# Turned keys in half a zeroed tile, z turned in five pieces, and another order of passes, scores and extra products

## The chip, the cores and the metric

The kernel runs on one core of one Trainium2 chip. The metric is the device time of one execution in microseconds. Names of the engines as the profile writes them: PE is TensorE (its weight loads are PEld), DVE is VectorE, ACT is ScalarE, POOL is GpSimd, and SP is SyncE, which here only issues DMAs.

## The reference

There are 8 batches of S = 3200 rows; u and v have D = 256 columns, z has 64. For every batch two stages follow each other:

```python
scores = (1.0 / S) * z @ z.T                 # S x S, symmetric
attn   = np.maximum(scores, 0.0) ** 2
x      = u * (attn @ v)                      # S x 256
wq, wk = x @ w_q, x @ w_k                    # S x 64 each
W_tok  = (1.0 / 8) * wq @ wk.T               # S x S, no nonlinearity
mixed  = W_tok @ x
out    = np.maximum(mixed, 0.0) @ w_out      # S x 256, float32
```

Since nothing stands between W_tok and x, the kernel computes wk.T @ x first (64 x 256, called the heads), and then wq times that.

## The kernel before

**Tiling.** The rows of a batch are 25 tiles of 128, put together in 7 groups: six of 512 rows and a last one of 128 (number 6, LASTG). For a group, the first stage makes score tiles (128 rows t by 512 columns of the group), squares them into fp16 tiles `at`, and multiplies them with v. As the scores are symmetric, a block that another group of the batch needs too is not computed again but turned by a transposing DMA (`tt`, `ttl`).

**Phases.** The main loop (`while groups`) runs through phases k = 0 to 164. An ordinary phase makes six score tiles, in three pairs, ahead of their use (LAG is two phases), and consumes some of the rows t of the current group: `second_product` lists the products that add up in two accumulator banks, acc0 and acc1. A group takes one to five phases. When it closes, `gate` multiplies the banks with u to give x and has x turned by a DMA. The last group of a batch is "split": its rows are shared out to the two banks, whose sum is taken in the gate (L391 to L393).

**Lanes.** Most phases run their products "on lanes" (`lanes`, L293 is where each product is emitted): the contraction over 128 rows is cut into a lower and an upper half of 64 rows, and two products, one from each half of PE, run side by side. A pass goes once through a set of products, with the lower lane in one bank and the upper lane in the other; the second pass goes through them with the lanes changed round. Between the passes `swap_after` waits for the ends of the first.

**PSUM.** There are the two accumulator banks and a pool of three tiles of two banks each ("ps"), which serves score pairs (sc), products for keys (qk), mixing products (mx) and projections (fo). The pool hands out the slot that was given back first. A slot is free again when the engines that read it are done.

**Score pairs.** A pair is evicted with ReLU by DVE (L243) or ACT (L239) into g, and g is squared into `at` by POOL (L258) or ACT (L256) in the next phase. In a phase the first two pairs stand at the head ("head scores") and the last one stands between the first and the second passes ("between score", `between_`).

**Extra products.** A phase can carry one extra:

- A key product (`keys_and_heads`): w_q and w_k times the turned x of a group, into the first bank of a qk tile, and beside it, in the second bank, the heads: turned keys of the group before (kx) times its x. ACT casts the first bank to fp16 (L432), SP issues the DMA that turns the keys (`turn_keys`), and DVE adds the heads to their sum (`heads_out`, L478 to L487). At the end of a batch the last two groups go together (a second cast, ql). A product of the batch before for its last 128 rows can go along as a "side product" (`aside`), read by ACT into rs or fs (L622, L641).
- A projection (`project`): mixed times w_out, evicted by ACT (L598) and written out.

`key_due` says when a key product may run, `mix_due` when a mixing product may. In a phase in which a group begins, the extra's first pass comes ahead of the banks' first pass; in others behind it. Its second pass comes ahead of the banks' second pass in both.

**Keys.** The DMA writes the turned keys into one half of a kx tile (128 rows x 4 x 2 x 64); POOL copies that half into the other (L454, `double_keys`), so that the heads come out twice, on partitions 0 to 63 and on 64 to 127. The copy is issued on POOL in the phase of the next key product, ahead of that phase's squares. The mixing products take the heads from both halves of the partitions.

**z.** For the next batch, POOL's queue loads z, DVE doubles it (`double_z`), and one transposing DMA, issued on SP, turns all 25 tiles (`turn_z`).

**Order.** Every engine runs its instructions in the order in which the program emits them; nothing is rescheduled. SP issues all transposing DMAs, the loads of u and the stores, POOL's queue loads z and v.

Of the kernel before, what the change touches and what calls it, by code (L numbers as in the profile page):

```python
# [9 lines left out]
FP16 = mybir.dt.float16  # L10
FP32 = mybir.dt.float32
# [5 lines left out]
def kernel(  # L17
# [10 lines left out]
    nc = tc.nc  # L28

    B, S, D = u.shape  # L30
    dqk = z.shape[2]
    dh = moe_w_q.shape[1]
# [21 lines left out]
    pzt = ctx.enter_context(tc.tile_pool(name="pzt", bufs=2))  # L54
    pv = ctx.enter_context(tc.tile_pool(name="pv", bufs=2))
    px = ctx.enter_context(tc.tile_pool(name="px", bufs=5))
    pk = ctx.enter_context(tc.tile_pool(name="pk", bufs=3))
    pxt = ctx.enter_context(tc.tile_pool(name="pxt", bufs=3))
    pu = ctx.enter_context(tc.tile_pool(name="pu", bufs=2))
    pg = ctx.enter_context(tc.tile_pool(name="pg", bufs=8))  # L60
# [36 lines left out]
    def load_first_v(n0, nn):  # L97
        nc.gpsimd.dma_start(out=vs[0][:, n0 : n0 + nn, :], in_=rows(v, 0)[:, n0 : n0 + nn, :])
# [34 lines left out]
    def double_z(b):  # L133
        nc.vector.tensor_copy(out=zds[b][:, :, 1, :], in_=zds[b][:, :, 0, :])

    def turn_z(b):
        zT[b] = pzt.tile([P, S], FP16, tag="zT2", name="zT2")
        nc.sync.dma_start_transpose(
            out=zT[b][:].rearrange("p (n s) -> p n s", s=P),
            in_=zds.pop(b)[:].rearrange("p n a k -> p (n a k)"),  # L140
        )

    def load_u(b, gi):
# [9 lines left out]
    wk2 = consts.tile([P, ND, 2, dh], FP32, tag="wk2", name="wk2")  # L153
    wo = consts.tile([P, ND, D], FP16, tag="wo", name="wo")
    zeros = consts.tile([P, D], FP16, tag="zeros", name="zeros")
    raw = {}

    def load_weights():
# [4 lines left out]
        nc.sync.dma_start(out=raw["k"], in_=moe_w_k.rearrange("(c p) h -> p c h", p=P))  # L163
        nc.sync.dma_start(out=raw["o"][:], in_=moe_w_out.rearrange("(c p) e -> p c e", p=P))

    def cast_weights():
        nc.gpsimd.tensor_copy(out=wqk[:, :, 0, :], in_=raw["q"])
        nc.gpsimd.tensor_copy(out=wqk[:, :, 1, :], in_=raw["k"])
        nc.gpsimd.tensor_copy(out=wkq[:, :, 1, :], in_=raw["q"])
        nc.gpsimd.tensor_copy(out=wkq[:, :, 0, :], in_=raw["k"])  # L170
        nc.gpsimd.memset(zeros[:], 0.0)
        for tile_ in hz:
            nc.gpsimd.memset(tile_[0:dh, :], 0.0)
        for half in range(2):
            nc.gpsimd.tensor_copy(out=wq2[:, :, half, :], in_=raw["q"])
            nc.gpsimd.tensor_copy(out=wk2[:, :, half, :], in_=raw["k"])
        nc.gpsimd.tensor_copy(out=wo[:], in_=raw["o"][:])

    LASTG = NG - 1

# [197 lines left out]
    def gate(b, gi):  # L383
        nn = widths[gi] // P
        xs[b, gi] = px.tile([P, 4, D], FP16, tag="x_sb", name="x_sb")
        x = xs[b, gi][:].rearrange("p n d -> p (n d)")
        ug = us.pop((b, gi))[:].rearrange("p n d -> p (n d)")
        n = min(2, nn) * D
        if is_split(b, gi):
            both = pg.tile([P, W], FP32, tag="g", name="gt")  # L390
            nc.scalar.copy(out=both[:, 0:n], in_=accs[1][:, 0:n])  # L391
            nc.vector.tensor_add(out=both[:, 0:n], in0=accs[0][:, 0:n], in1=both[:, 0:n])
            nc.vector.tensor_mul(out=x[:, 0:n], in0=both[:, 0:n], in1=ug[:, 0:n])  # L393
        else:
            if nn > 2:
                upper = pg.tile([P, W], FP32, tag="g", name="gt")
                nc.scalar.copy(out=upper[:], in_=accs[1][:])  # L397
            nc.vector.tensor_mul(out=x[:, 0:n], in0=accs[0][:, 0:n], in1=ug[:, 0:n])  # L398
            if nn > 2:
                nc.vector.tensor_mul(out=x[:, n : 2 * n], in0=upper[:], in1=ug[:, n : 2 * n])  # L400
        turn_x(b, gi)
# [32 lines left out]
    def turn_keys(b, gi):  # L434
        gw = widths[gi]
        mine = slice(0, dh) if swapped(gi) else slice(dh, P)
        ks[b, gi] = pk.tile([P, 4, 2, dh], FP16, tag="kx", name="kx")
        nc.sync.dma_start_transpose(
            out=ks[b, gi][:, 0 : gw // P, 1, :],
            in_=qks[b, gi][mine, 0:gw],  # L440
        )

    doubled = set()

    def double_keyed():
        hb, hgis = keyed[0]
        for g_ in hgis:
            if (hb, g_) not in doubled:
                doubled.add((hb, g_))
                double_keys(hb, g_)  # L450

    def double_keys(b, gi):
        nn = widths[gi] // P
        nc.gpsimd.tensor_copy(out=ks[b, gi][:, 0:nn, 0, :], in_=ks[b, gi][:, 0:nn, 1, :])  # L454

    def swapped(gi):
        return gi % 2 == 1 or gi == LASTG
# [15 lines left out]
    def heads_out(b, gis, ps):  # L475
        if gis[0] == 0:
            hacc[b] = psml.tile([P, D], FP32, tag="ha", name="ha")
            nc.vector.tensor_copy(out=hacc[b][:], in_=ps[:, 1, 0:D])  # L478
        elif gis[-1] < LASTG:
            nc.vector.tensor_add(out=hacc[b][:], in0=hacc[b][:], in1=ps[:, 1, 0:D])  # L480
        else:
            heads_done(b, ps[:, 1, 0:D])
            nc.vector.tensor_copy(out=hz[b % 2][dh:P, :], in_=hss[b][dh:P, :])

    def heads_done(b, part):
        hss[b] = psml.tile([P, D], FP16, tag="hs", name="hs")
        nc.vector.tensor_add(out=hss[b][:], in0=hacc.pop(b)[:], in1=part)  # L487

    def last_gram(b, gi, ps):
        nj = widths[gi] // P  # L490
# [158 lines left out]
    def due(k, fn):  # L649
        at_phase.setdefault(k, []).append(fn)  # L650
# [53 lines left out]
    def group_begun(k, b, gi):  # L704
        if gi + 1 < NG:
            due(k + 1, lambda: load_u(b, gi + 1))
        elif b + 1 < B:
            due(k + 1, lambda: load_u(b + 1, 0))
        if gi == 0 and b + 1 < B:
            later = 4 if b == 0 else 0  # L710
            due(k + later + 3, lambda: load_z(b + 1))
            due(k + later + 9, lambda: double_z(b + 1))
            due(k + later + 10, lambda: turn_z(b + 1))
            for i in range(5):
                due(k + later + 5 + 3 * i, lambda i=i: load_v(b + 1, 5 * i, 5))

# [3 lines left out]
    make_identity(nc, ident)  # L720
    load_first_z()
    load_first_v(0, 4)
    cast_first(0)
    turn_first(0)
    cast_first(1)
# [3 lines left out]
    load_first_v(18, 7)  # L729
    load_first_v(4, 8)  # L730
    due(3, lambda: load_u(0, 0))
    due(5, load_weights)
    due(8, cast_weights)

    def mix_due(k):
        if todo_mix and todo_mix[0][2] == 0 and len(todo_proj) > 2:
# [4 lines left out]
        return (older or len(todo_mix) > 2) and k - mixed_at[0] >= 2 and not key_due(k)  # L741

    def key_due(k):
        between_ = 2 if len(groups) > NG else 1
        return todo_between and todo_between[0][0] <= k and k - keyed_at[0] > between_

    made_by = []
    waiting = []
# [4 lines left out]
    while groups:  # L753
# [16 lines left out]
        n = min(n, NTILE - produced)  # L770
        pairs = list(range(produced, produced + n, 2))
        on_lanes = k >= 3 and len(pairs) + bool(mixing) >= 2
        between_ = [pairs.pop()] if on_lanes else []
        fresh = [(p0, scores(p0)) for p0 in pairs]
        produced += n
        made_by.append(produced)
        keying = not mixing and key_due(k)
        if keying and keyed:
            double_keyed()
        if mixing:  # L780
            mix_out(*mixing)
        staged = []
# [29 lines left out]
            continue  # L812
        ready = made_by[k - (1 if k < 3 else LAG)]
        b, gi = groups[0]
        begins = left is None
        if begins:
            group_begun(k, b, gi)
            need = ends[b, gi]
# [23 lines left out]
        extra = None  # L842
        if keying:
            extra = todo_between.pop(0)[1]()
        elif todo_proj and (mixing or begins or len(groups) <= NG) and (b, gi) != (last, LASTG):
            extra = project(*todo_proj.pop(0))
        if mixing and mixing[2] == 1:
            todo_proj.extend((mixing[0], 2 * mixing[1] + a) for a in range(2))
        if on_lanes:
            split = is_split(b, gi)  # L850
            if extra and not all(extra[0]):
                for fn in whole(extra[0]):
                    fn()
                extra[1]()
                extra = None
            if extra and begins:
                ends_ = lanes(extra[0], across, False)
            if split:
                both_lanes(banks)
            else:  # L860
                ends_ = lanes(banks, across, False)
            if extra and not begins:
                ends_ = lanes(extra[0], across, False)
            for x in acts[1:]:
                second_stage(*x)
            for p0 in between_:
                stage(p0, scores(p0))
            if extra or not split:
                swap_after(ends_)
                across = not across  # L870
            if extra:
                lanes(extra[0], across, True)
                extra[1]()
            if not split:
                lanes(banks, across, True)
        else:
            assert not is_split(b, gi)
            matmuls = whole(banks)
            cut = 10 if extra else 0
            if closes and (b, gi) == (last, LASTG):  # L880
                assert not extra
                cut = 20
                psg = [acc_tile(1, "xtx")[:, 0:D], ps_tile("xtx")[:, 0, 0:D]]
                extra = [], lambda: last_gram(last, LASTG - 1, psg)
            for fn in matmuls[:cut]:
                fn()
            if extra:
                for fn in whole(extra[0]):
                    fn()
                extra[1]()  # L890
            for x in acts[1:]:
                second_stage(*x)
            for fn in matmuls[cut:]:
                fn()
# [22 lines left out]

    halves = [(True, nc.sync, 2), (True, nc.sync, 2)]

    double_keyed()  # L920
    hb, hgis = keyed.pop()
    psh = ps_tile("hd")
    for fn in whole([heads(hb, hgis, psh, stop=False)]):
# [60 lines left out]
```

## Time and profile before

| | |
|---|---|
| time, three runs | 800.03, 806.02, 813.67 us (median 806.02) |
| time of the profiled execution | 810.74 us |
| its span, first to last instruction | 809.0 us |
| mean granted clock of PE | 0.994 |
| PE busy | 770.5 us, 95% |
| DVE, ACT, POOL busy | 506.1, 485.3, 481.3 us |
| DMA moved | 141.70 MB, mean 175 GB/s |
| transposing DMAs issued on SP (tt, xT, kx, zT) | 162, 56, 47, 7 for the larger kinds |

"Busy" is the time in which the engine has an instruction under way. Matmuls are pipelined and their ends are modelled, so 95% means that PE hardly ever stops, not that its array is full. The groups of instructions give the source line, the engine, the operation, the tile written and the one read, the shape, the number of them, their busy time and the mean of one in ns, and behind the bar the time that the engine stood idle just before them, with what released it. A line of the timeline gives the start and the length in us, and in brackets the wait before it.

### The profile page before, as it was taken

What the parts mean: (1) busy time and instruction counts of PE and PEld (TensorE: products, weight loads), DVE (VectorE), ACT (ScalarE), POOL (GpSimd) and SP (SyncE); (2) the same over time, 40 slices, a digit from 0 to 9 for tenths busy, and PEclk for the clock granted to TensorE, in tenths of its full rate; (3) what the DMA queues carried; (4) which work ended last, traced back from release to release, by engine and by line L of the source; (5) the groups of instructions that cost most, each with busy time, mean ns of one, the idle gap of its engine ahead of it and who ended that gap; (6) DMA issues with size and microseconds to landing.
All of it is one profiled execution on the core that took longest, in us unless ns stands there. A gap on an engine that the chain in (4) does not pass through costs nothing. (4 is left out here: it accounts for less than half of the span.)

```text
span 809.0 us, 27835 instructions
## 1 busy us (share of the span) xinstructions
PE 770.5 (95%) x12338; PEld 624.5 (77%) x12338; DVE 506.1 (63%) x516; ACT 485.3 (60%) x569; POOL 481.3 (59%) x351
## 2 busy tenths in 40 slices
PE   7889999999999999899999899999999989999996
PEld 4667877887788778788778677878878868778884
DVE  5765567656676567655767556765567645676524
ACT  6654566557576557555666546755666645665634
POOL 7865677646765567645676365663767545766520
PEclk9999999999999999999999999999999999999999
DMA  8999799999999969999899969999999995999826
GB/s 161 159 186 195 142 169 173 182 175 158 192 176 214 160 138 186 161 198 227 162 190 174 190 135 177 155 187 222 188 195 160 184 183 132 194 188 161 194 55 229
DMA packets 331159, 141.70 MB, mean 175 GB/s; under 512 B 310560, under 2 KB 313248, under 8 KB 331040
## 3 DMA queue, kind: packets, MB, share of 16 engines
q1 hardware_dynamic: 302768, 123.70, 83.5%
q0 software_dynamic: 28128, 15.98, 17.6%
q8 instruction: 96, 1.57, 0.8%
q10 hardware_dynamic: 144, 0.26, 0.1%
q14 instruction: 23, 0.19, 0.1%
HBM read 59.38 MB, written 26.21 MB: 106 GB/s over the span
## 5 line engine op out<-in xcount | busy, mean ns | idle before, releaser
L258 POOL TENSOR_TENSOR at<-g 128x1024 f16<-128x1024 f32 (+1 forms) x228 | 421.7, 1857 | 204.7 <-DVE g L243 148.6
L243 DVE TENSOR_SCALAR g<-sc 128x1024 f32<-128x1024 f32 (+1 forms) x330 | 389.3, 1187 | 235.0 <-PE sc L220 230.2
L293 PE MATMUL acc<-v_sb,at 64*128 64x256 f16 (+1 forms) x6995 | 443.3, 270 | 8.1 <-DVE x_sb L398 2.5
L293 PEld LDWEIGHTS <-at 64*128 64x128 f16 (+1 forms) x6995 | 353.7, 94 | 89.9 <-PE acc L293 17.0
L256 ACT ACTIVATE at<-g 128x1024 f16<-128x1024 f32 (+2 forms) x224 | 224.5, 1031 | 1.5 <-DMA ttl<-at 0.9
L239 ACT ACTIVATE g<-sc 128x1024 f32<-128x1024 f32 x122 | 125.2, 1026 | 115.8 <-PE sc L220 115.7
L293 PE MATMUL acc<-v_sb,tt 64*128 64x256 f16 (+1 forms) x2528 | 170.2, 270 | 0.0
L220 PE MATMUL sc<-zT 64*128 64x512 f16 x888 | 154.4, 380 | 5.6 <-DVE g L243 4.2
L293 PEld LDWEIGHTS <-tt 64*128 64x128 f16 (+1 forms) x2528 | 128.1, 94 | 12.8
L454 POOL COPY kx<-kx 128x256 f16<-128x256 f16 (+1 forms) x54 | 22.5, 421 | 94.0 <-DMA kx<-qk 90.3
L397 ACT COPY gt<-acc 128x512 f32<-128x512 f32 x48 | 28.1, 585 | 71.4 <-PE acc L293 68.9
L293 PE MATMUL qk<-x_sb,kx 64*128 64x256 f16 x378 | 57.8, 275 | 11.4 <-POOL kx L454 11.4
L598 ACT ACTIVATE fo<-fo 128x1024 f32<-128x1024 f32 (+2 forms) x44 | 43.7, 999 | 34.5 <-PE fo L293 34.0
L537 ACT ACTIVATE rt<-mx 128x1024 f16<-128x1024 f32 x47 | 47.9, 1025 | 25.4 <-PE mx L516 23.5
L432 ACT CAST qk<-qk 128x512 f16<-128x512 f32 x47 | 27.5, 584 | 54.5 <-PE qk L293 54.0
L220 PEld LDWEIGHTS <-zT 64*128 64x128 f16 x888 | 49.7, 94 | 13.4 <-issue 6.8
L293 PE MATMUL fo<-wo,rt 64*128 64x256 f16 (+1 forms) x704 | 56.9, 271 | 0.1
L398 DVE TENSOR_TENSOR x_sb<-acc,u_sb 128x512 f16<-128x512 f32 (+1 forms) x49 | 33.6, 686 | 37.3 <-PE acc L293 36.5
L293 PEld LDWEIGHTS <-kx 64*128 64x128 f16 (+1 forms) x382 | 32.1, 95 | 23.1 <-POOL kx L454 14.3
L293 PEld LDWEIGHTS <-rt 64*128 64x128 f16 (+1 forms) x704 | 34.8, 94 | 18.4 <-PE acc L293 4.4
L400 DVE TENSOR_TENSOR x_sb<-gt,u_sb 128x512 f16<-128x512 f32 x48 | 43.0, 895 | 2.4 <-ACT gt L397 2.2
L293 PE MATMUL qk<-xT_sb,wqk 64*128 64x512 f16 (+1 forms) x92 | 32.7, 395 | 1.6 <-DMA xT_sb<-x_sb 1.6
(68 smaller groups left out, 269.6 us busy)
## 6 DMA issues: line engine op xcount, KB each, us to landing
u_sb<-in_u_dram SPq DMA_DIRECT2D x48, 512.0 KB, 5.0
out_dram<-fo SPq DMA_DIRECT2D x45, 512.0 KB, 4.1
v_sb<-in_v_dram POOLq DMA_DIRECT2D x35, 320.0 KB, 5.5
zd<-in_z_dram POOLq DMA_DIRECT2D x7, 400.0 KB, 10.7
tt<-at SPq DMA_TRANSPOSE x162, 4.9
out_dram<-fo SPq DMA_DIRECT2D x5, 256.0 KB, 2.7
u_sb<-in_u_dram SPq DMA_DIRECT2D x8, 128.0 KB, 3.6
xT_sb<-x_sb SPq DMA_TRANSPOSE x56, 4.5
```

What stands on the lines that cost most here:

```text
L220: nc.tensor.matmul(out=sc[:, h, :], lhsT=zT[b][half : half + dqk, ts(ti, P)], rhs=zT[b][half : half + dqk, ds(gs, W)], start=True, stop=True,)
L239: nc.scalar.activation(out=g[:, hs, 0:w], in_=sc[:, hs, W - w : W], func=RELU, scale=GSCALE)
L243: nc.vector.tensor_scalar(out=g[:, hs, 0:w], in0=sc[:, hs, W - w : W], scalar1=0.0, scalar2=GSCALE, op0=AOP.max, op1=AOP.mult,)
L256: nc.scalar.square(out=out, in_=g[:, hs, 0:w])
L258: nc.gpsimd.tensor_mul(out=out, in0=g[:, hs, 0:w], in1=g[:, hs, 0:w])
L293: return nc.tensor.matmul(out=self.out, lhsT=self.lhsT(rows), rhs=self.rhs(rows), start=start, stop=stop)
L397: nc.scalar.copy(out=upper[:], in_=accs[1][:])
L398: nc.vector.tensor_mul(out=x[:, 0:n], in0=accs[0][:, 0:n], in1=ug[:, 0:n])
L400: nc.vector.tensor_mul(out=x[:, n : 2 * n], in0=upper[:], in1=ug[:, n : 2 * n])
L432: nc.scalar.copy(out=qks[b, gi][:, 0:gw], in_=out)
L537: nc.scalar.activation(out=out, in_=ps[:], func=RELU)
L598: nc.scalar.mul(out=flat_out[:, sl], in_=part, mul=FINAL_SCALE)
```

## The change

- `turn_keys`: three fixed kx tiles are set to zero once, at the start. The DMA writes the turned keys into half 0 of a tile, and half 1 stays zero. The copy on POOL is gone. The heads then come out on partitions 0 to 63 alone; the running sum is kept there, and DVE copies the finished one, `hs`, to partitions 64 to 127, once a batch.
- `turn_z`: five DMAs of five tiles each, in five phases in a row, take the place of one.
- The weights are loaded in phase 4 instead of 5, and their casts on POOL are spread over phases 8, 10, 11 and 13.
- The gate of a split group has DVE copy acc0 into SBUF, and adds from there.
- `key_due` and the choice of projections follow other conditions.
- Ordinary phases with no extra and no group start have one head pair and two between pairs; a mixing phase without extra has none and two.
- On lanes, all first passes come first, then the between scores, then the second passes in the same order as the first. So in a phase in which a group begins the extra is ahead in both; in any other it is behind the banks in both. In a split group the first ten rows of both banks come ahead of the between scores and the others behind them.

```diff
-    def turn_z(b):
-        zT[b] = pzt.tile([P, S], FP16, tag="zT2", name="zT2")
+    def turn_z(b, n0, nn):
+        if n0 == 0:
+            zT[b] = pzt.tile([P, S], FP16, tag="zT2", name="zT2")
         nc.sync.dma_start_transpose(
-            out=zT[b][:].rearrange("p (n s) -> p n s", s=P),
-            in_=zds.pop(b)[:].rearrange("p n a k -> p (n a k)"),
+            out=zT[b][:].rearrange("p (n s) -> p n s", s=P)[:, n0 : n0 + nn, :],
+            in_=zds[b][:, n0 : n0 + nn, :, :].rearrange("p n a k -> p (n a k)"),
         )
...
+    kxs = [pk.tile([P, 4, 2, dh], FP16, tag=f"kx{i}", name=f"kx{i}") for i in range(3)]
...
+    def clear():
+        for tile_ in [zeros] + kxs:
+            nc.gpsimd.memset(tile_[:], 0.0)
...
-            both = pg.tile([P, W], FP32, tag="g", name="gt")
-            nc.scalar.copy(out=both[:, 0:n], in_=accs[1][:, 0:n])
-            nc.vector.tensor_add(out=both[:, 0:n], in0=accs[0][:, 0:n], in1=both[:, 0:n])
-            nc.vector.tensor_mul(out=x[:, 0:n], in0=both[:, 0:n], in1=ug[:, 0:n])
+            both = pg.tile([P, 2, W], FP32, tag="g", name="gt")
+            nc.scalar.copy(out=both[:, 1, 0:n], in_=accs[1][:, 0:n])
+            nc.vector.tensor_copy(out=both[:, 0, 0:n], in_=accs[0][:, 0:n])
+            nc.vector.tensor_add(out=both[:, 0, 0:n], in0=both[:, 0, 0:n], in1=both[:, 1, 0:n])
+            nc.vector.tensor_mul(out=x[:, 0:n], in0=both[:, 0, 0:n], in1=ug[:, 0:n])
...
-        ks[b, gi] = pk.tile([P, 4, 2, dh], FP16, tag="kx", name="kx")
+        kxs.append(kxs.pop(0))
+        ks[b, gi] = kxs[-1]
         nc.sync.dma_start_transpose(
-            out=ks[b, gi][:, 0 : gw // P, 1, :],
+            out=ks[b, gi][:, 0 : gw // P, 0, :],
...
-    def double_keys(b, gi):
-        nn = widths[gi] // P
-        nc.gpsimd.tensor_copy(out=ks[b, gi][:, 0:nn, 0, :], in_=ks[b, gi][:, 0:nn, 1, :])
...
-        nc.vector.tensor_add(out=hss[b][:], in0=hacc.pop(b)[:], in1=part)
+        nc.vector.tensor_add(out=hss[b][0:dh, :], in0=hacc.pop(b)[0:dh, :], in1=part[0:dh, :])
+        nc.vector.tensor_copy(out=hss[b][dh:P, :], in_=hss[b][0:dh, :])
...
-            due(k + later + 10, lambda: turn_z(b + 1))
+            for i in range(5):
+                due(k + later + 10 + i, lambda i=i: turn_z(b + 1, 5 * i, 5))
...
     def key_due(k):
-        between_ = 2 if len(groups) > NG else 1
-        return todo_between and todo_between[0][0] <= k and k - keyed_at[0] > between_
+        late = len(groups) <= NG
+        if not todo_between or k - keyed_at[0] <= (1 if late else 2):
+            return False
+        ready = todo_between[0][0]
+        if late or todo_proj:
+            return ready <= k
+        if left is None:
+            return ready - 1 <= k
+        return ready <= k and not (len(sizes) < 3 and k + len(sizes) - ready < 3)
...
-        between_ = [pairs.pop()] if on_lanes else []
+        keying = not mixing and key_due(k)
+        begins = left is None
+        projecting = not keying and todo_proj and groups[0] != (last, LASTG) and (
+            begins or len(todo_proj) > (1 if mixing else 2) or len(groups) <= NG
+        )
+        heading = len(pairs)
+        if on_lanes:
+            heading = heading - 1 if begins or keying or projecting else 1 - bool(mixing)
+        between_ = pairs[heading:]
+        pairs = pairs[:heading]
...
-            if extra and begins:
-                ends_ = lanes(extra[0], across, False)
-            if split:
-                both_lanes(banks)
-            else:
-                ends_ = lanes(banks, across, False)
-            if extra and not begins:
-                ends_ = lanes(extra[0], across, False)
+            parts = [] if split else [banks]
+            if extra:
+                parts.insert(0 if begins else len(parts), extra[0])
+            cut = 10
+            firsts = [lanes(part, across, False) for part in parts]
+            if split:
+                both_lanes([bank[:cut] for bank in banks])
             for x in acts[1:]:
                 second_stage(*x)
             for p0 in between_:
                 stage(p0, scores(p0))
-            if extra or not split:
+            if split:
+                both_lanes([bank[cut:] for bank in banks])
+            if parts:
+                across = not across
+            for part, ends_ in zip(parts, firsts):
                 swap_after(ends_)
-                across = not across
-            if extra:
-                lanes(extra[0], across, True)
-                extra[1]()
-            if not split:
-                lanes(banks, across, True)
+                lanes(part, across, True)
+                if extra and part is extra[0]:
+                    extra[1]()
```

More of the change, by code (lines that the diff above doesn't have):

```diff
@@ L56 @@
     px = ctx.enter_context(tc.tile_pool(name="px", bufs=5))
-    pk = ctx.enter_context(tc.tile_pool(name="pk", bufs=3))
+    pk = ctx.enter_context(tc.tile_pool(name="pk", bufs=1))
     pxt = ctx.enter_context(tc.tile_pool(name="pxt", bufs=3))
@@ L164, in load_weights @@
         nc.sync.dma_start(out=raw["o"][:], in_=moe_w_out.rearrange("(c p) e -> p c e", p=P))
+    def clear():
+        for tile_ in [zeros] + kxs:
+            nc.gpsimd.memset(tile_[:], 0.0)
+        for tile_ in hz:
+            nc.gpsimd.memset(tile_[0:dh, :], 0.0)
     def cast_weights():
@@ L170, in cast_weights, with double_weights, cast_out_weights @@
         nc.gpsimd.tensor_copy(out=wkq[:, :, 0, :], in_=raw["k"])
[L171 to L176, printed above, removed]
+    def double_weights(half):
+        nc.gpsimd.tensor_copy(out=wq2[:, :, half, :], in_=raw["q"])
+        nc.gpsimd.tensor_copy(out=wk2[:, :, half, :], in_=raw["k"])
+    def cast_out_weights():
         nc.gpsimd.tensor_copy(out=wo[:], in_=raw["o"][:])
@@ L436, in turn_keys @@
         mine = slice(0, dh) if swapped(gi) else slice(dh, P)
-        ks[b, gi] = pk.tile([P, 4, 2, dh], FP16, tag="kx", name="kx")
+        kxs.append(kxs.pop(0))
+        ks[b, gi] = kxs[-1]
         nc.sync.dma_start_transpose(
-            out=ks[b, gi][:, 0 : gw // P, 1, :],
+            out=ks[b, gi][:, 0 : gw // P, 0, :],
             in_=qks[b, gi][mine, 0:gw],
         )
[L443 to L450, printed above, removed]
-    def double_keys(b, gi):
-        nn = widths[gi] // P
-        nc.gpsimd.tensor_copy(out=ks[b, gi][:, 0:nn, 0, :], in_=ks[b, gi][:, 0:nn, 1, :])
     def swapped(gi):
@@ L477, in heads_out @@
             hacc[b] = psml.tile([P, D], FP32, tag="ha", name="ha")
-            nc.vector.tensor_copy(out=hacc[b][:], in_=ps[:, 1, 0:D])
+            nc.vector.tensor_copy(out=hacc[b][0:dh, :], in_=ps[0:dh, 1, 0:D])
         elif gis[-1] < LASTG:
-            nc.vector.tensor_add(out=hacc[b][:], in0=hacc[b][:], in1=ps[:, 1, 0:D])
+            nc.vector.tensor_add(
+                out=hacc[b][0:dh, :], in0=hacc[b][0:dh, :], in1=ps[0:dh, 1, 0:D]
+            )
         else:
             heads_done(b, ps[:, 1, 0:D])
-            nc.vector.tensor_copy(out=hz[b % 2][dh:P, :], in_=hss[b][dh:P, :])
+            nc.vector.tensor_copy(out=hz[b % 2][dh:P, :], in_=hss[b][0:dh, :])
     def heads_done(b, part):
         hss[b] = psml.tile([P, D], FP16, tag="hs", name="hs")
-        nc.vector.tensor_add(out=hss[b][:], in0=hacc.pop(b)[:], in1=part)
+        nc.vector.tensor_add(out=hss[b][0:dh, :], in0=hacc.pop(b)[0:dh, :], in1=part[0:dh, :])
+        nc.vector.tensor_copy(out=hss[b][dh:P, :], in_=hss[b][0:dh, :])
     def last_gram(b, gi, ps):
@@ L722 @@
     load_first_v(0, 4)
+    clear()
     cast_first(0)
@@ L731 @@
     due(3, lambda: load_u(0, 0))
-    due(5, load_weights)
+    due(4, load_weights)
     due(8, cast_weights)
+    due(10, lambda: double_weights(0))
+    due(11, lambda: double_weights(1))
+    due(13, cast_out_weights)
     def mix_due(k):
@@ L772 @@
         on_lanes = k >= 3 and len(pairs) + bool(mixing) >= 2
-        between_ = [pairs.pop()] if on_lanes else []
+        keying = not mixing and key_due(k)
+        begins = left is None
+        projecting = not keying and todo_proj and groups[0] != (last, LASTG) and (
+            begins or len(todo_proj) > (1 if mixing else 2) or len(groups) <= NG
+        )
+        heading = len(pairs)
[3 more added lines that the diff above has]
+        pairs = pairs[:heading]
         fresh = [(p0, scores(p0)) for p0 in pairs]
@@ L776 @@
         made_by.append(produced)
-        keying = not mixing and key_due(k)
-        if keying and keyed:
-            double_keyed()
         if mixing:
@@ L814 @@
         b, gi = groups[0]
-        begins = left is None
         if begins:
@@ L844 @@
             extra = todo_between.pop(0)[1]()
-        elif todo_proj and (mixing or begins or len(groups) <= NG) and (b, gi) != (last, LASTG):
+        elif projecting:
             extra = project(*todo_proj.pop(0))
```

1 line of the change is left out of this document (removed).

## The prediction, made before the changed kernel was run

> **What bounds the kernel now.** I read the busy shares first, then the table of waits, then stretches of the timeline.
>
> ```profile
> PE 770.5 (95%) x12338; PEld 624.5 (77%) x12338; DVE 506.1 (63%) x516; ACT 485.3 (60%) x569; POOL 481.3 (59%) x351
> ...
> DMA  8999799999999969999899969999999995999826
> ```
>
> TensorE (PE) is the bound (the DMA row, busy tenths in 40 slices, comes back under rival 3). Two lanes finish a product of 256 columns every 0.109 us; at that pace the products need 749 us of the 799 us between the first and the last. The other 50 us are pauses, and only what makes or removes a pause of PE counts. In the table of waits (who waits for whom: total us, times, longest):
>
> ```profile
> POOL kx L454 <- DMA kx<-qk: 90.3, 21, 10.9
> ...
> ACT gt L397 <- PE acc L293: 68.9, 46, 4.2
> ...
> PE qk L293 <- POOL kx L454: 11.4, 8, 2.8
> ...
> PE sc L220 <- DVE g L243: 4.2, 6, 0.7
> ```
>
> The first row is large and free: POOL waits, PE doesn't. PE's own waits are the last two rows, some 0.5 us at each of the 16 group starts that have no extra product ahead of them (8 us: the closed banks' gate copies), and the start-up (3.8 us, below). Measured gap by gap on PE, the waits for keys are 12.9 us at eight places (1.44 to 3.0 us at five, 0.38 to 0.65 at three), and the waits for a score slot 0.83 us at six places, 5.0 us.
>
> The timeline around a key product shows what a score tile's slot needs to come free:
>
> ```profile
> 237.93 0.38 PE L293 MATMUL qk<-xT_sb,wqk 64*128 64x512 f16 x1
> 238.04 0.27 PE L293 MATMUL qk<-x_sb,kx 64*128 64x256 f16 x1
> 238.15 1.47 PE L293 MATMUL acc<-v_sb,at 64*128 64x256 f16 x24
> 238.35 0.58 ACT L432 CAST qk<-qk 128x512 f16<-128x512 f32 x1
> 238.99 0.41 DVE L487 TENSOR_TENSOR hs<-ha,qk 128x256 f16<-128x256 f32 x1
> ```
>
> The product ends at 238.31; ScalarE starts 0.04 later and takes 0.58; VectorE starts 0.06 after that and takes 0.41. So the slot is free 1.09 us after the product's end (E), and PE can start 0.05 later. Meanwhile PE works on the banks' second pass (the third row), so nothing is lost. That cover is what the change moves.
>
> **The change, part by part.**
>
> *Second passes in another order.* Before, the extra product's second pass came ahead of the banks' second pass, which then covered its eviction (1.3 to 2.8 us in ordinary phases). After, where the phase begins no group, the extra's second pass comes last. Three tiles share the score slots, and they are given out in the order in which they were freed, so the next phase's extra takes the slot of this one. If that phase begins a group, its extra starts right behind two head scores (0.44 us of work), about 0.28 us after E by the modelled ends; it must wait for the eviction. The added prices come from these rows:
>
> ```profile
> L598 ACT ACTIVATE fo<-fo 128x1024 f32<-128x1024 f32 x42 | 43.0, 1023 | 34.5 <-PE fo L293 34.0 <-ACT at L256 0.5
> L432 ACT CAST qk<-qk 128x512 f16<-128x512 f32 x47 | 27.5, 584 | 54.5 <-PE qk L293 54.0
> L480 DVE TENSOR_TENSOR ha<-ha,qk 128x256 f32<-128x256 f32 x31 | 12.9, 416 | 10.6 <-ACT qk L432 8.9 <-ACT ql L432 0.9
> L622 ACT ACTIVATE rs<-qk 128x256 f16<-128x256 f32 x7 | 2.7, 383 | 3.4 <-DVE ha L478 3.4
> ```
>
> A key product: 0.04+0.584+0.05+0.416+0.05 = 1.14, less 0.28 = 0.86 us. With the short last group's keys ScalarE has two casts (127.25 to 128.00 at one such place): 0.04+0.75+0.03+0.42+0.05-0.28 = 1.01 us. With the 128-row side product, 0.383 and a hand-over of 0.05 more: 1.29 us. A projection: 0.04+1.023+0.05-0.28 = 0.83 us. The changed order of instructions gives these places: 9 with a side product (11.6), 2 with short keys (2.0), 6 plain (5.2), 7 projections and one at 1.05 (6.9), three behind a short last group (2.5) and one mixing phase (1.0). Sum: **+29.2 us** at 29 places. From below: if only half of each shows, +15; from above, ScalarE is in a square of 1.05 us at a quarter of them when the product ends, +8 more.
>
> *Split gate and between-scores.* A split group's products after the tenth now stand behind the between-score, so its eviction has work of PE beside it before the next phase's scores need the slot: the six waits of 0.83 us go, **-5.0**. A new VectorE copy of acc0 (0.42 like the 128x256 rows) runs beside ScalarE's copy and frees acc0 at about E+0.46 instead of E+0.88; that wait showed once, 1.2 us: **-1.2**. Group starts without an extra fall from 16 to 12 at 0.5 us: **-2.0**.
>
> *Keys.* 54 POOL copies go (22.7 us busy, and the 94 us of waiting before them). POOL is no bound, but at the eight late places copy and hand-over (0.5) stood on the path: -4. Against that, key products lie closer: from a key product's end to the first use of its keys PE has about 10.8 us of work at the median instead of 12.9. The median key transfer lands 6.5 us after the product, the longest 11.9 to 16.4; three of these sit right behind the one long turn of z, which is now five short ones. The new pauses above also give the transfers time. I take **-6.4**, half of the wait; ends -12.9 (all gone) and +13 (eight late places, each 2.1 us later less 0.5).
>
> *z in five pieces.* 35 issues instead of 7 on SP. An issue of this size takes about 1.2 us (the other transposes), one long one 3.9 to 5.3: 35x1.2-7x4.5 = some 10 us of SP time spread over 35 phases. Behind them stand tt, xT and key transposes, a 1.2 us delay each at most; 0 taken, ends 0 and +5. Scores of the next batch now wait per piece, with 1 to 2 us of slack.
>
> *Small things.* Three memsets of 128x512 on POOL at the start (311 ns for 128x256; about 0.5 each) lie in 1.8 us of its idle time. Eight 64x256 copies double hs on VectorE (the like copy to hz takes 1.14 us): 9 us on an engine busy 63%; the mix that reads hs comes two phases later. Zero taken, ends 0 and +3. PE's products are the same multiset.
>
> *Start-up.* The first key product moves from phase 11 to 10.
>
> ```profile
> 48.98 0.60 PE L293 MATMUL qk<-xT_sb,wqk 128*128 128x512 f16 x2 [1.61 <-DMA xT_sb<-x_sb]
> ```
>
> Before, it waited 1.8 us for the turned x, which SP issued only at 41.3 since it had transposes without a break from 19.4. After, the POOL wait at 37.9 (2.0 us, behind the weight casts) is gone, so PE is there at about 40.5, but x still lands at 47.5 to 48.9: a pause of some 7.5 us. -2.0-1.8+7.5 = +3.7. A long pause also costs clock:
>
> ```profile
> 465.24 0.31 PE L293 MATMUL qk<-x_sb,kx 64*128 64x256 f16 x1 [2.82 <-POOL kx L454]
> ```
> ```profile
> 465.00:469.00 4.00, 3.76 (x34) 2.56 (x36) 1.22 (x1) 0.58 (x1) 3.89 (x3) 0.57 1.03 180
> ```
>
> After 2.8 us without work the granted clock (third number from the end) is 0.57 over 4 us, a loss of 0.43x4 = 1.7 us; after 1.6 us (at 49) it stays 1.00. So **+5.4**; ends -3.8 and +9.
>
> [...]
>
> Sum: +29.2-5.0-1.2-2.0-6.4+5.4 = **+20 us** on the profiled 810.7, which lies 4.7 above the median: 831 in a profile like that one, **826 us** at the median of 806.
>
> **Rivals.** (1) *The pauses pay for other waits.* What PE waits at the evictions, it no longer waits for keys or turned x: all 12.9 goes, and start-up costs nothing: 826-6.5-5.4 = 814. For it: transfers run on in the pauses. Against: the late keys and the pauses are at different phases.
>
> (2) *Faster: no eviction wait.* If the extra found its slot free (the 29.2 under some 9 us, its deciding point), the gains remain: 826-29.2 = 797, and with all key waits and no start-up loss 785. For it: ScalarE idles 54 us before these casts, so it is prompt. Against: slots are reused in order, and PE waited the full 0.83 at each of the six like places of before.
>
> (3) *Keys later.* The shorter windows (10.8 us) meet transfers of 12 to 16 us; six to ten more waits of 2 to 3 us, some with clock loss: +16, 842. For: the DMA engines are at 90% and more in most slices. Against: only a few transfers are that long.
>
> (4) *Readers side by side.* The cast reads the tile's first bank and the add its second. In before the add never starts ahead of the cast's end, in all 31 places, so the program orders them; if after did not, the key waits would shrink by 0.42 to 0.52 each, 8 us in all: 818.
>
> [...] The trace shows the chip's engines one behind the other here, so the sum goes by the trace.
>
> **Chances.** Forecast 0.50 (816 to 836), rivals 1 and 4 together 0.27 (806 to 820), rival 2 0.10, rival 3 0.13. Two per cent is about what a measurement can tell here (three runs spread from 800 to 814): 790 and 822. Of the forecast's half 0.42 lies above 822; with rival 3 slower is 0.55; faster takes 0.07 of rival 2; the rest, 0.38, is the same. The range 803 to 842 leaves out most of rival 2 and half of rival 3.
>
> **What would show it.** PE waits for ScalarE or VectorE ahead of qk and fo products, some 28 of them, 0.8 to 1.3 us each; no PE wait for scores behind split groups; POOL without kx copies; a pause of over 5 us near 41 followed by half clock; PE's busy time unchanged. I am wrong if the eviction waits sum to under 15 us, or if waits on key transfers grow past 20.

## The result, and the profile after

| | before | after |
|---|---|---|
| first comparison, median of four runs | 804.45 us | 844.3 us, ratio 1.0503 (95%: 1.0411 to 1.0595) |
| second comparison, same kernels on another occasion | 807.15 us | 839.73 us, ratio 1.0414 (1.0346 to 1.0481) |

The change makes the kernel slower by 4 to 5%, some 33 to 40 us. The forecast was 826 us, with 842 at the upper end: the first comparison lies above that end, the second just under it. One of the four first runs, the profiled one, took 2059.51 us, each product twice as long as in all others (0.534 us for 256 columns against 0.270); no other run of this study did that. The median of the four has it in, the ratio leaves it out; without it the median is 842.7 us. The profile of after is therefore that of the second comparison (839.96 us; its span 838.2).

The page of after, its first lines:

```profile
span 838.2 us, 27778 instructions
## 1 busy us (share of the span) xinstructions
PE 770.4 (92%) x12338; PEld 676.7 (81%) x12338; DVE 502.7 (60%) x531; ACT 482.8 (58%) x570; POOL 467.3 (56%) x299
```

PE is busy as long as before (770.4 against 770.5 us); the 29 us more of span are pauses. PE's rows of the table of waits in after (who waits for whom: total us, times, longest):

```profile
PE qk L296 <- DMA kx<-qk: 14.3, 4, 6.5
PE fo L296 <- ACT rs L615: 5.7, 5, 1.2
PE fo L296 <- DVE ha L470: 5.3, 7, 0.9
...
PE fo L296 <- ACT fs L634: 4.6, 4, 1.1
PE qk L296 <- DMA xT_sb<-x_sb: 4.5, 1, 4.5
PE qk L296 <- ACT fo L591: 4.1, 6, 0.7
```

Four of these rows are new: projections (fo) wait for the three readers of a qk tile (rs, ha, fs), and key products for the reader of a projection (fo). The scores' wait for g, six times before, shows once. The waits for keys have not gone: POOL is no longer their releaser, the DMA is, and they are fewer but longer (14.3 us at four places, where it was 11.4 at eight).

I summed the pauses of PE of over 0.1 us in the two profiles, measured against two lanes of 0.109 us per 256 columns:

| pauses of PE, us | before | after | forecast of the difference | measured |
|---|---|---|---|---|
| an extra waits for a slot (fo, qk) | 0 | 28.3 at 29 places | +29.2 | +28.3 |
| a score waits for a slot | 5.3 | 0.9 | -5.0 | -4.4 |
| keys late | 12.9 | 15.0 | -6.4 | +2.1 |
| gates at group starts | 9.7 | 11.8 | -3.2 | +2.1 |
| start-up (from 32 us on) | 3.8 | 4.6 | +3.7 | +0.9 |
| mixing products | 0.2 | 1.9 | 0 | +1.7 |
| the rest: small gaps, and products at a lower clock (0.21 us apart instead of 0.109, as at 465 in before and 225 in after) | 10.7 | 7.7 | +1.7 | -3.0 |
| sum | 42.6 | 70.2 | +20.0 | +27.7 |

The rest up to 29.2 is mostly PE's first product, which comes 1.4 us later. The profiled execution of before (810.74 us) was slower than its medians and that of after (839.96) was not, so the table accounts for 29 of the 33 to 40 us; where the others lie no profile shows.

One of the 29 places, at a group start in after (all engines, weight loads left out):

```profile
178.34 0.27 PE L296 MATMUL qk<-ql,hz 64*128 64x128 f16 x2
178.45 0.59 PE L223 MATMUL sc<-zT 64*128 64x512 f16 x4
178.70 0.59 ACT L436 CAST qk<-qk 128x512 f16<-128x512 f32 x1 [5.05 <-PE qk L296]
179.32 0.42 DVE L468 COPY ha<-qk 64x256 f32<-64x256 f32 x1 [2.74 <-ACT qk L436]
...
179.77 0.38 ACT L615 ACTIVATE rs<-qk 128x256 f16<-128x256 f32 x1 [0.48 <-DVE ha L468]
...
180.20 0.61 PE L296 MATMUL fo<-wo,rt 64*128 64x256 f16 x8 [1.16 <-ACT rs L615]
```

The key product with its side product ends last in its phase, at 178.66. PE makes two score pairs and stops. Cast, copy and side eviction follow one another, and 0.05 us after the last of them the projection starts. Counted over both lanes the pause is 1.31 us; 1.29 had been worked out.

One of the two long waits for keys, first PE, then SP, which issues the DMAs:

```profile
218.07 0.37 PE L296 MATMUL qk<-xT_sb,wqk 64*128 64x512 f16 x1 [0.69 <-ACT fo L591]
224.93 0.39 PE L296 MATMUL qk<-x_sb,kx 64*128 64x256 f16 x1 [6.48 <-DMA kx<-qk]
```
```profile
209.14 1.94 SPq L410 DMA_TRANSPOSE xT_sb<-x_sb  x1
211.12 0.58 SPq L147 DMA_DIRECT2D u_sb<-in_u_dram  x1
211.81 1.37 SPq L280 DMA_TRANSPOSE tt<-at  x1
213.60 1.78 SPq L280 DMA_TRANSPOSE ttl<-at  x1
215.45 0.60 SPq L147 DMA_DIRECT2D u_sb<-in_u_dram  x1
216.15 1.21 SPq L443 DMA_TRANSPOSE kx<-qk  x1
```

The keys' product ended at 209.11. Its transfer is issued only at 216.15, behind five others, and lands 15.8 us after the product: 7.0 us pass ahead of the issue and 8.7 from there to the landing. The next key product already runs at 218.07, 9 us behind. Before, the key product of the same phase, 42, had 20 us (203.05 to 223.13), since the next came five phases later and not three, and its transfer landed after 6.6 us. So two things changed: the window became shorter, and the transfer landed later. With the landing of before, 9 us would have been enough. Clock is lost as well: behind this wait the granted clock was 0.73 over 5 us, and behind the one at the start-up 0.68. The view by stretches of after (the third number from the end is the granted clock):

```profile
225.00:230.00 5.00, 5.00 (x64) 4.03 (x66) 1.48 (x2) 1.09 (x2) 0.00 (x0) 0.73 1.22 218
45.00:50.00 5.00, 3.81 (x34) 2.53 (x36) 0.00 (x0) 2.49 (x3) 0.40 (x1) 0.68 1.35 238
```

### The profile page after: what moved, and what is told of

Read it like the earlier page. It is cut to its first block, busy times and chain, and to the rows that moved or that the text cites. A ratio compares the mean times of both kernels' runs of the same rounds, so it can differ in the third digit from the quotient of the medians.

```text
span 2057.7 us, 27778 instructions
## 1 busy us (share of the span) xinstructions
PE 2041.8 (99%) x12338; PEld 1142.8 (56%) x12338; DVE 498.2 (24%) x531; ACT 485.7 (24%) x570; POOL 466.0 (23%) x299
## 4 chain that ended last, share of the span: by engine, by line
PE 98%; ACT 1%; DVE 0%; issue 0%; DMA 0%; DVEq 0%
PE acc L296 72%; PE sc L223 12%; PE qk L296 6%; PE fo L296 6%; PE mx L509 1%; ACT qk L436 0%; PE ztp L118 0%; PE xtx L486 0%; DVE ha L470 0%; PE hd L496 0%; DMA z<-in_z_dram 0%; DVE ha L468 0%; ACT rs L615 0%; DVE zd L109 0%; ACT fs L634 0%
## 5 line engine op out<-in xcount | busy, mean ns | idle before, releaser
L296 PE MATMUL acc<-v_sb,at 64*128 64x256 f16 (+1 forms) x6995 | 1128.9, 534 | 0.9 <-DVE x_sb L402 0.7
L296 PEld LDWEIGHTS <-at 64*128 64x128 f16 (+1 forms) x6995 | 644.1, 172 | 516.1 <-issue 119.3
L261 POOL TENSOR_TENSOR at<-g 128x1024 f16<-128x1024 f32 (+2 forms) x227 | 425.5, 1875 | 1515.0 <-DVE g L246 1023.1
L296 PE MATMUL acc<-v_sb,tt 64*128 64x256 f16 (+1 forms) x2528 | 425.6, 534 | 0.0
L223 PE MATMUL sc<-zT 64*128 64x512 f16 x888 | 343.2, 834 | 1.4 <-ACT zT L122 0.9
L296 PEld LDWEIGHTS <-tt 64*128 64x128 f16 (+1 forms) x2528 | 229.3, 172 | 152.8
L259 ACT ACTIVATE at<-g 128x1024 f16<-128x1024 f32 (+1 forms) x225 | 223.7, 1022 | 16.9 <-DVE g L246 16.4
L296 PE MATMUL fo<-wo,rt 64*128 64x256 f16 (+1 forms) x704 | 132.0, 520 | 3.9 <-ACT rs L615 2.0
L296 PE MATMUL qk<-x_sb,kx 64*128 64x256 f16 x378 | 134.1, 533 | 0.0
L296 PE MATMUL qk<-xT_sb,wkq 64*128 64x512 f16 (+1 forms) x120 | 71.5, 723 | 0.0
```

Source lines behind the costliest of these rows:

```text
L223: nc.tensor.matmul(out=sc[:, h, :], lhsT=zT[b][half : half + dqk, ts(ti, P)], rhs=zT[b][half : half + dqk, ds(gs, W)], start=True, stop=True,)
L259: nc.scalar.square(out=out, in_=g[:, hs, 0:w])
L261: nc.gpsimd.tensor_mul(out=out, in0=g[:, hs, 0:w], in1=g[:, hs, 0:w])
L296: return nc.tensor.matmul(out=self.out, lhsT=self.lhsT(rows), rhs=self.rhs(rows), start=start, stop=stop)
```

## The experiments

Each ratio is to the kernel before, run beside it, with its 95% interval.

### The changed kernel again

> The changed kernel, unaltered, for a second profile, since the first profiled execution took 2059.5 us with products of 0.534 us and isn't like the others (839.65 to 848.32). Theory A (eviction waits of the extra products): the time is 838 to 848, PE waits for ScalarE or VectorE ahead of qk and fo products at some 29 places, 30 to 40 us in all, waits for keys stay under 13. Theory B (keys in shorter windows): PE's waits for key transfers are 20 us or more, with half clock behind several of them, and the eviction waits are under 15.

839.73 us, 1.0414 (1.0346 to 1.0481). Theory A has its places and their sum, 28.3 us. Theory B is not out: the late keys cost 15.0 us, more than the 13 that A allowed.

### Order of the second passes, in the changed kernel

```diff
-            for part, ends_ in zip(parts, firsts):
+            seconds_ = list(zip(parts, firsts))
+            if extra and not begins:
+                seconds_.reverse()
+            for part, ends_ in seconds_:
```

> The changed kernel, but in phases in which no group begins the extra's second pass is put ahead of the banks' second pass again; nothing else is altered. Theory A: the eviction waits get their cover back, 29 to 38 us less than the changed kernel: 806 to 815. Theory B: the keys come as late as before this edit or later, at most 10 us less: 834 or more.

821.25 us, 1.0167 (1.0097 to 1.0236): 18.5 us less, where A said 29 to 38 and B at most 10. The waits for slots fall from 28.3 us to 3.6, those of the projections among them from 22.8 to 1.4, so the mechanism is right. But the first row of the waits grows:

```profile
PE qk L296 <- DMA kx<-qk: 20.2, 7, 8.0
PE qk L296 <- DMA xT_sb<-x_sb: 5.3, 1, 5.3
```

It was 14.3 us at four places. The pauses had given the key transfers time, as I read it; when they go, part of it comes back as waits for keys, and the mean clock of this profile is 0.981.

### The same order, in the kernel before

```diff
-            if extra:
+            if extra and begins:
                 lanes(extra[0], across, True)
                 extra[1]()
             if not split:
                 lanes(banks, across, True)
+            if extra and not begins:
+                lanes(extra[0], across, True)
+                extra[1]()
```

> The kernel before with one edit: in phases in which no group begins the extra's second pass comes behind the banks' second pass. Theory A: most of the loss by this alone, 25 to 35 us: 829 to 839. Theory B: the key product ends later by the length of the banks' second pass (some 2 us), so its keys do; with windows of 12.9 us at the median that gives 5 to 10 us: 809 to 814.

823.47 us, 1.0221 (1.0152 to 1.029): 16 us, between A and B. In the old schedule of keys only a few phases with an extra stand ahead of a group start with another. In the profile (span 820.4 against 809.0) PE waits 6.9 us more for projections' slots at six places, 1.15 each, and some 4 us more for closed banks.

### The keys part alone

```diff
-        nc.gpsimd.tensor_copy(out=ks[b, gi][:, 0:nn, 0, :], in_=ks[b, gi][:, 0:nn, 1, :])
+        pass
...
+        kxs.append(kxs.pop(0))
+        ks[b, gi] = kxs[-1]
...
+        nc.vector.tensor_copy(out=hss[b][dh:P, :], in_=hss[b][0:dh, :])
```

> The kernel before with the keys part alone: zeroed kx tiles, no copy on POOL, sums on 64 partitions, hs doubled once a batch. Both theories: the eight waits for keys lose the copy and its hand-over, 4 us: 800. If POOL's squares, queued behind the copies, had held up PE somewhere, up to 12 less: 792. If the copy was hidden after all: 804.

802.42 us, 0.9952 (0.9915 to 0.999). Some 4 us less, as worked out from the copy and its hand-over; the waits for keys fall from 12.9 to some 8.5 us. POOL's 94 us of waiting were free, as the forecast had it.

### The old schedule of keys, with both orders

```diff
     def key_due(k):
+        between_ = 2 if len(groups) > NG else 1
+        return todo_between and todo_between[0][0] <= k and k - keyed_at[0] > between_
```

This takes the place of the new body. The second kernel has the reversed second passes too.

> The changed kernel with the condition for key products (key_due) of the kernel before; all else, the extra's second pass at the end among it, stays. Theory A (the loss is made by the order of second passes together with the new schedule of keys, which puts an extra ahead of a group start that has one too, 28 times): with the old schedule 9 such places are left, some 9 us; the start-up and the two waits of 6 to 7 us for keys go: 806 to 814. Rival C (the passes' order, the two between pairs or the z pieces cost by themselves, whatever the schedule): 824 or more.

> Both edits: the old key_due, and the extra's second pass ahead of the banks' where no group begins. Theory A: neither late keys nor eviction waits are left, the gains of the split group and the keys without copies remain: 796 to 803. Rival C: 810 or more.

818.27 us, 1.0138 (1.0099 to 1.0177), 4 us above A's range and 6 below C's; and 807.19 us, 0.998 (0.9931 to 1.0029), no different from before, where A had hoped for 796 to 803 and C for 810 or more. The profile of the first shows where A was too hopeful: PE still waits 14.4 us for slots, at 17 places instead of 9, and for keys it has the rows

```profile
PE qk L296 <- DMA kx<-qk: 7.8, 6, 2.7
PE qk L296 <- DMA kx<-ql: 2.4, 2, 1.5
```

The two long waits of after, 6.6 and 5.7 us, are gone, but others have come. Gap by gap, and against after, the waits for slots fall from 28.3 to 14.4 us, the start-up from 4.6 to 0.7 and the keys from 15.0 to 11.9, of 21.6 us of span. With the other order of second passes the schedule acts on the keys most of all: 21.3 us with the new one, 10.4 with the old. Together with the two kernels above this makes a square:

| | extra's second pass last | extra's second pass first |
|---|---|---|
| new schedule of keys | 839.7 (1.041) | 821.3 (1.017) |
| old schedule of keys | 818.3 (1.014) | 807.2 (0.998) |

The order costs 11 us with the old schedule and 18 with the new; the schedule costs 14 with one order and 21 with the other. Either alone is a small loss. Together they cost 32.5, 7 more than their sum. The schedule puts more extras ahead of group starts that have one, which would make the two add up to more; but each of the four ratios has an interval of 0.4 to 0.7% to either side, and the rows come from two occasions, so that these 7 us are not shown. What else is in the change (five pieces, score pairs, split group, weights) adds up to nothing that can be told: the corner without the two is the kernel before in time.

### z in five pieces

```diff
+            for i in range(5):
+                due(k + later + 10 + i, lambda i=i: turn_z(b + 1, 5 * i, 5))
```

This is on top of the keys part; it ran on two occasions.

> The kernel before with the keys part, and z turned in five pieces on top. If the pieces neither gain nor lose: 802.4 as the keys part alone, within 3. If 10 us more of SP issue time delays transposes that PE waits for: 806 or more. If the three late keys behind the long turn of z are on time: 797 to 799.

> The base of the two, the kernel before with the keys part and z in five pieces, again on the same chip, so that they can be compared: 801 to 802, or 0.985 to 0.99 of the kernel before.

801.57 us, 0.9868 (0.9799 to 0.9937), and 803.38 us, 1.0017 (0.9985 to 1.0049). The two intervals don't meet, so a ratio of this study can differ by some 1.5% from occasion to occasion; smaller gains, that of the keys part among them, are not sure from one occasion. The pieces cost nothing that can be seen. In their two profiles PE waits 3.9 and 5.7 us for keys, where the keys part alone had some 8.5; whether that gains a few us of time stays open.

### The split group in two parts

```diff
+            cut = 10
+            if split:
+                both_lanes([bank[:cut] for bank in banks])
...
             for p0 in between_:
                 stage(p0, scores(p0))
+            if split:
+                both_lanes([bank[cut:] for bank in banks])
```

On top of the keys part, with the gate of after.

> The kernel before with the keys part, and on top the split group cut behind ten rows with the between score there, and the gate with a VectorE copy of acc0. Theory: the six waits of 0.83 us for a score slot and the 1.2 us gate wait go: 802.4 less 6 is 796. If the wait only moves on to the next eviction: 802.

805.58 us, 0.9941 (0.99 to 0.9983), the same as the keys part alone (0.9952). The wait moved on, as the waits of this kernel show:

```profile
PE qk L298 <- ACT fo L606: 4.1, 6, 0.7
```

Six times 0.83 us for a score slot became six times 0.85 us for the slot of the projection that the next key product asks for.

Next came the order that should cover both: four rows, the between score, the extra's second pass, the other rows.

```diff
+            cut = 4
+            if split:
+                both_lanes([bank[:cut] for bank in banks])
...
             if extra:
                 lanes(extra[0], across, True)
                 extra[1]()
-            if not split:
+            if split:
+                both_lanes([bank[cut:] for bank in banks])
+            else:
                 lanes(banks, across, True)
```

> The kernel before with the keys part and z in five pieces, and on top a split group in another order: four rows of both banks, the between score, the extra's second pass, and then the other rows, which cover both evictions. In the cut at ten rows the wait for a score slot went and one of 0.85 us for the slot of a projection came, at the same six places. If the other rows cover both: 5 us less than the base of 801.6, 796 to 797. If the wait moves on once more: 801 to 802.

> The same, and the weights loaded in phase 4 with their casts on POOL spread over phases 8 to 13. If POOL's casts stood on the path at 37.9 us: 1 to 2 us less than without. If the first key product then waits longer for the turned x: no difference.

803.15 us, 0.9981 (0.9944 to 1.0019), and with the weights spread 801.49 us, 0.9964 (0.9926 to 1.0003), against 1.0017 for their base. In the first, scores wait 2.4 us instead of 5.2, and no projection's slot is waited for; but the waits for keys are 7.7 us, where the base had 4.3. Neither edit can be told from no change.

### One head pair ahead of an extra

```diff
             heading = heading - 1 if begins or keying or projecting else 1 - bool(mixing)
+            if begins and (keying or projecting):
+                heading = 1 - bool(mixing)
```

> The changed kernel with one edit: in a phase in which a group begins and that has an extra, one score pair stands at the head and two between the passes, instead of two and one. The extra is then the second and not the third to ask for a score slot, and gets that of the last between pair, evicted long before; the slot of the extra before goes to a between score, behind the banks' first pass. Order of passes and key schedule stay. Theory A (the wait is for that one slot): nearly all of the eviction waits go, 15 to 25 us less than 840: 815 to 825, as with the extra's second pass ahead. Rival D (the wait is for the engines behind, whatever slot is taken): 835 or more.

848.14 us, 1.0552 (1.0486 to 1.0618): worse than after, as D has it and not A. The waits of PE in this kernel:

```profile
PE acc L296 <- DVE x_sb L402: 20.2, 22, 1.4
PE qk L296 <- DMA kx<-qk: 16.8, 4, 6.7
PE acc L296 <- ACT gt L401: 10.2, 14, 1.4
```

No extra waits for a slot any more, so A names the slot rightly. But the time stays lost: the banks that closed with the phase now hold PE, 44.3 us of pauses ahead of acc products against 11.8. The timeline of this kernel at the same group start as above tells why:

```profile
183.38 0.60 PE L296 MATMUL fo<-wo,rt 64*128 64x256 f16 x8
183.42 0.59 ACT L436 CAST qk<-qk 128x512 f16<-128x512 f32 x1 [5.05 <-PE qk L296]
...
184.03 0.42 DVE L468 COPY ha<-qk 64x256 f32<-64x256 f32 x1 [2.74 <-ACT qk L436]
184.38 0.67 DVE L402 TENSOR_TENSOR x_sb<-acc,u_sb 128x512 f16<-128x512 f32 x1
184.48 0.39 ACT L615 ACTIVATE rs<-qk 128x256 f16<-128x256 f32 x1 [0.48 <-DVE ha L468]
184.76 0.58 ACT L401 COPY gt<-acc 128x512 f32<-128x512 f32 x1
185.19 1.67 PE L296 MATMUL acc<-v_sb,at 64*128 64x256 f16 x24 [1.21 <-DVE x_sb L402]
```

The extra's eviction was emitted ahead of the gate. The gate's copy and product queue behind it on ACT and DVE (184.76 and 184.38), so the banks come free later than the extra's tile: PE goes on with acc at 185.19, 1.21 us late. In after the pause for the slot hid this second one.

## Why the prediction was wrong

The direction was right, the time was not: 20 us were forecast and 33 to 40 came. In the two profiles the pauses grew by 27.7 us: the keys cost 8.5 us more than forecast and the gates 5.3, and the start-up, the eviction waits and the small gaps some 6 less. By its own steps:

**"Second passes in another order", +29.2 at 29 places: right.** 28.3 us at 29 places were measured, singly 0.84 for projections, 0.87 for plain keys and 1.27 to 1.31 with a side product. The reason, slots reused in order, was shown by the kernel with one head pair, which made these waits vanish. The step did not see that the closed banks are nearly as late.

**"Keys", -6.4: wrong, and the largest miss.** The step took a median window of 10.8 us against a median landing of 6.5 us, and gave the pauses of the new order credit for the transfers. Two places decide instead, phases 42 and 124: there the next key product comes some 9 us after the last, where it had 20, and the transfer, queued on SP behind five others, lands after 15 to 16 us, where it landed after 6 to 7. These two cost 12.4 us, so that keys cost 2.1 us more in all instead of 6.4 less. The bound of +13 held the value. With the old schedule put back these two waits go, so they hang on the schedule. But with the order of after the waits for keys are only 3 of the 21 us that this gives back, and most of the others are waits for slots; with the other order they are 11 of 14. Why the two transfers land so much later stays open beyond the 7.0 us that each stands ahead of its issue.

**"Group starts without an extra", -2.0, and the split gate, -1.2: wrong.** Pauses at the banks rose by 2.1 us. The split gates make most of that, 4.3 us against 2.4. The forecast let ScalarE's copy of the other bank start as the group ends; at four of the seven split groups ACT evicts an extra first, as here:

```profile
200.63 1.02 ACT L591 ACTIVATE fo<-fo 128x1024 f32<-128x1024 f32 x1 [0.81 <-PE fo L296]
201.55 0.37 ACT L394 COPY gt<-acc 128x256 f32<-128x256 f32 x1
201.96 1.27 PE L296 MATMUL acc<-v_sb,at 64*128 64x256 f16 x20 [0.87 <-ACT gt L394]
```

The other group starts have 7.5 us, against 7.3 before, where 2.0 less had been forecast; this is not traced further.

**"Split gate and between-scores", -5.0: removed, but hardly gained.** Scores wait 4.4 us less. In the kernel with this part alone the six waits came back at the next key product, 0.85 us each. In after, three of the seven split groups have a wait for a slot right behind them, as many as the forecast had counted, and the other four the wait for the gate just told.

**Start-up, +5.4: too high.** The pause was 4.6 us and not 7.5, as x was turned by 46.1 and not by 47.5; the granted clock behind it was 0.68 over 5 us, a loss of 1.6 us where 1.7 had been forecast.

**z pieces and the small things at nothing: held**, as far as the square's last corner and the two occasions with the pieces tell.

Of the rivals, *keys later* was nearest in time (842), with its mechanism at two places rather than at six to ten. *The pauses pay for other waits* has its share: without the pauses the waits for keys grew from 14.3 to 20.2 us. *No eviction wait* is refuted. So is *readers side by side*: cast, copy and side eviction ran one behind the other in after too (178.70, 179.32 and 179.77 at the place above). In the first profile of after VectorE starts on the heads behind the cast's end at all 46 places, 0.02 to 0.04 us behind it.

## What to carry to other kernels

Count the work that stands between the last product into a tile and the next use of its slot, and do it for all that closes at the same point: with a slot and two banks given back together, taking one wait away only uncovered the next here (0.83 us became 0.85; 1.31 became 1.37). Judge a transfer by the latest one against the shortest window, not by two medians; here two of 54 transfers made 12.4 of the 15.0 us. Where two edits act on the same waits, the schedule and the order here, try them as a square: each alone cost 11 to 14 us here, and only the fourth kernel tells whether the two add up.

## What was not expected of the hardware

The copies of 64x256 fp16 on DVE took longer where POOL had a product under way beside them. In before the hz copies took 0.224 us at the two places without a POOL product beside them, and 1.02 to 1.70 us at the five with one; at these five the copy ends 0.07 to 0.1 us after POOL's product does. In after the seven took 0.21 to 0.32, and the new hs copies 0.459 in the mean (0.933 in the kernel with the keys part alone): two of the eight stand beside a POOL product, with 1.70 and 0.65 us, and the six others take 0.22. The row of after:

```profile
L480 DVE COPY hs<-hs 64x256 f16<-64x256 f16 x8 | 3.7, 459 | 0.3
```

What holds the copies up no trace here shows. The add of the heads on 64 partitions was hardly shorter than on 128 (411 ns in after against 416 in before).
